# Start addresses of TensorE's streamed and loaded tiles, set by paddings in the second feed-forward network

## The chip, the cores and the metric

The kernel runs on one core of a Trainium2 chip. The metric is the time that the device takes for one execution, in microseconds (us). Smaller is better. The time of the kernel before is the median of three runs, 2021.54 us (2019.42 to 2022.19).

## The reference

Three stages follow one another. The input is 4 sequences of 3072 tokens with 256 channels, in float32.

```python
X = rfft(x, axis=1)                                   # 1: mixing along the sequence
Yr = Xr @ w_r - Xi @ w_i + b_r;  Yi = Xr @ w_i + Xi @ w_r + b_i
Y = soft_threshold(Yr, 0.01) + 1j * soft_threshold(Yi, 0.01)
y = irfft(Y, n=3072, axis=1)
xk, xr = mu * y + (1 - mu) * shifted(y)               # 2: first feed-forward network, 256 -> 1024 -> 256
out = sigmoid(xr @ w_rr) * (relu(xk @ w_k) ** 2 @ w_v)
h = out @ w_in                                        # 3: second feed-forward network, 256 -> 2048 -> 256
result = (h * clip(h + 3, 0, 6) / 6) @ w_out
```

## The kernel before

**How products are made.** A product of two float32 matrices is made of three matmuls: each operand is held as a rounded high part and the rest, a low part (names end in h and l, or in _hi and _lo), and high*high, low*high and high*low are added up in PSUM. A matmul consists of a weight load (LDWEIGHTS, 128 x 128 values of the operand that stays in the array) and the matmul proper (MATMUL), in which the other operand streams through, 256 or 512 columns. The load of the next matmul's weights runs beside the current matmul. So what is read at the same time is the streamed tile of one matmul and the weight tile of the one behind it.

**The stages in order.** Up to about 740 us the Fourier mixing (matmuls named s, mix, ia, ib) runs, from about 180 us on mixed with the first network (pr, pk, acc). From 740 us to 1000 us the first network runs alone, with the decoding of the second network's weights beside it. From 1000 us on the second network runs: its first tile of 512 tokens (of 24) with plain products (pi, 512 columns), and from 1043 us on 23 tiles by a scheme that replaces 8 block products by 7 (`u_s`: rq and cc, 256 columns), while the product with w_out (`u_o`: oacc, 256 columns) of an earlier unit is put in between.

**A turn of the second network.** A tile has 8 units; each turn (`turn`) advances four units in a fixed order. TensorE's part of a turn is 12 matmuls whose weights are sums of w_in (tiles sw0, sw1), then 9 whose weights are w_in itself (wi_hi, wi_lo), then the 24 matmuls of `u_o`, whose weights are the activations gh and gl and whose streamed tiles are wo_hi and wo_lo. What streams in the first 21 are the parts of the tile of tokens (xh, xl, allocated under the tags kh and kl, and the combinations th and tl). ScalarE and VectorE make a unit's gh and gl in its fourth turn, and `u_o` reads them in the turn after that. The order of all engines' work is written out by hand.

**Where tiles begin.** SBUF is handed out by pools in the order of the code; a pool takes a tile's place when the tile's tag is first used, and `pad` takes a few bytes with no use. Buffers of one tag, slices and halves that a matmul reads all lie whole multiples of 256 bytes apart, so one number, the address modulo 256, tells where all of a tag's operands begin. In the program before:

| read by | streamed tile: begins at | weight tile: begins at |
|---|---|---|
| mix (Fourier) | aw: 224 | Xh, Xl: 32 |
| ia (Fourier) | yh, yl: 224 | tt: 32 |
| pr, pk (first network) | kh, kl: 32 | wr, wk: 32 |
| acc (first network) | gh, gl: 32 | wv: 32 |
| pi (second network, first tile) | xh, xl (tags kh, kl): 32 | wi: 96 |
| rq, first 12 of a turn | xh, xl (tags kh, kl), th, tl: 32 | sw0, sw1: 32 |
| rq, cc, next 9 of a turn | xh, xl, th, tl: 32 | wi: 96 |
| oacc, 24 of a turn | wo: 224 | gh, gl: 32 |

The change touches `prep` (L536, the first use of the tags kh and kl), `split_s` (L679 to L682) and the allocation of the second network's weights (L967 to L971). All matmuls of the second network's later tiles are recorded under L824, those of pk, pr, acc, pi, mix and ia under L164.

Of the kernel before, what the change touches and what calls it, by code (L numbers as in the profile page):

```python
# [104 lines left out]
def fourier_mix_ffn_kernel(  # L105
# [33 lines left out]
    kb = ctx.enter_context(tc.tile_pool(name="kb", bufs=1))  # L139
# [5 lines left out]
    def pad(pool, n):  # L145

        pads.append(n)
        pool.tile([128, n // 4], F32, name=f"pad{len(pads)}")
# [73 lines left out]
    def decoder(jobs, stage):  # L222

        running = []
        for n in range(2 * len(jobs) + 5):
            for r in running:
                next(r, None)
            running = running[-3:]
            if n % 2 == 0 and n // 2 < len(jobs):
                w, *job = jobs[n // 2]  # L230
                running.append(w.decode(w.load(stage, *job), *job))
            yield
# [6 lines left out]
    with tc.manual_schedule(engines=order):  # L239
# [273 lines left out]
        def prep(i):  # L513

            if i:
                y = yt.pop(i)
                before, now = [(0, TOK, y)], [(0, TOK, y[:, :, N1:])]
            else:

                y1, y2 = ysb.pop(1), ysb.pop(2)  # L520
                before = [(0, 352, y1[:, :, 32:]), (352, TOK, y2)]
                now = [(0, 256, y1[:, :, 128:]), (256, TOK, y2)]
            for w in (1, 0):
                xf = kb.tile([128, 2, TOK], F32, tag="xf", bufs=1, name="xf")
                for a in range(2):
                    for lo, hi, y in before:
                        nc.scalar.activation(xf[:, a, lo:hi], y[:, a, 0 : hi - lo], AF.Copy, scale=omu[:, w, a : a + 1])
                yield
                for a in range(2):
                    for lo, hi, y in now:  # L530
                        o = xf[:, a, lo:hi]
                        nc.vector.scalar_tensor_tensor(
                            o, y[:, a, 0 : hi - lo], mus[:, w, a : a + 1], o, op0=ALU.mult, op1=ALU.add
                        )
                yield
                h = kb.tile([128, 2, TOK], F32R, tag="kh", bufs=3, name="kh")  # L536
                l = kb.tile([128, 2, TOK], F32R, tag="kl", bufs=3, name="kl")
                nc.scalar.activation(h, xf, AF.Copy)
                yield
                nc.vector.tensor_sub(l, xf, h.bitcast(F32))  # L540
                xs[i, w] = h, l
                yield

        def u_r(i):
            xr = xs.pop((i, 1))
            p = ptile("pr")
            for m in range(2):
                c = slice(128 * m, 128 * m + 128)
                three(
                    p[:, 512 * m : 512 * m + 512],  # L550
                    [((wr.hi[:, k, c], wr.lo[:, k, c]), (xr[0][:, k], xr[1][:, k])) for k in range(2)],
                )
            r = kb.tile([128, 2, TOK], F32, tag="r", bufs=2, name="r")
            nc.scalar.activation(r.rearrange("p a n -> p (a n)"), p, AF.Sigmoid)
            rs[i] = r

        def u_k(i, j):
            xk = xs[i, 0]
            p = ptile("pk")
            for m in range(2):  # L560
                c = slice(256 * j + 128 * m, 256 * j + 128 * m + 128)
                three(
                    p[:, 512 * m : 512 * m + 512],
                    [((wk.hi[:, k, c], wk.lo[:, k, c]), (xk[0][:, k], xk[1][:, k])) for k in range(2)],
                )
            g = kb.tile([128, 1024], F32, tag="g", bufs=2, name="g")
            h = kb.tile([128, 1024], F32R, tag="gh", bufs=3, name="gh")
            l = kb.tile([128, 1024], F32R, tag="gl", bufs=3, name="gl")
            nc.scalar.activation(g, p, AF.Relu)

            def rest():

                nc.scalar.activation(h, g, AF.Square)  # L573
                nc.vector.tensor_mul(g, g, g)  # L574
                nc.vector.tensor_sub(l, g, h.bitcast(F32))  # L575

            hv[i, j] = (h, l)
            return rest
# [95 lines left out]
        def split_s(sp, i):  # L674

            x = xt[i].rearrange("p k (t n) -> p k t n", t=2)
            flat = xt[i].rearrange("p k (t n) -> p (k t) n", t=2)
            tmp = {}
            h = kb.tile([128, 4, 256], F32R, tag="kh", bufs=3, name="xh4")  # L679
            l = kb.tile([128, 4, 256], F32R, tag="kl", bufs=3, name="xl4")  # L680
            th = sp.tile([128, 4, 256], F32R, tag="th", bufs=2, name="th")
            tl = sp.tile([128, 4, 256], F32R, tag="tl", bufs=2, name="tl")  # L682
            own = slice(0, 1), slice(2, 4)

            def four():
                t = tmp["t"] = sp.tile([128, 4, 256], F32, tag="t", bufs=1, name="xs")
                nc.vector.tensor_sub(t[:, 1], x[:, 0, 1], x[:, 0, 0])
                nc.vector.tensor_sub(t[:, 2], x[:, 1, 1], t[:, 1])
                nc.vector.tensor_sub(t[:, 3], x[:, 1, 1], x[:, 0, 1])
                nc.vector.tensor_sub(t[:, 0], x[:, 1, 0], t[:, 2])  # L690

            def high():
                for n in own:
                    nc.scalar.activation(h[:, n], flat[:, n], AF.Copy)

            def low():
                for n in own:
                    nc.vector.tensor_sub(l[:, n], flat[:, n], h[:, n].bitcast(F32))

            xt[i] = {n: (h[:, m], l[:, m]) for n, m in (("11", 0), ("21", 2), ("22", 3))}  # L700
            xt[i] |= {n: (th[:, m], tl[:, m]) for m, n in enumerate(("t4", "t1", "t2", "t3"))}
            return [
                (four, high),
                (low, lambda: nc.scalar.activation(th, tmp["t"], AF.Copy)),
                (lambda: nc.vector.tensor_sub(tl, tmp["t"], th.bitcast(F32)), None),  # L705
            ]
# [153 lines left out]
        for step, _ in enumerate(stream(first)):  # L860
# [4 lines left out]
            if step in SPLIT_MIX:  # L865
                w, staged, job = plain.pop(0)
# [4 lines left out]
            if step in DECODE:  # L871
                next(loads, None)
        fs = stream(later)
        preps = prep(0)
        for n in range(4):
            next(preps)
# [12 lines left out]
        def feed():  # L889

            nonlocal live_f
            live_f = live_f and next(fs, 0) is None
# [10 lines left out]
        def decode_to(n):  # L903

            nonlocal done2
            while done2 < n:
                next(jobs2, None)
                done2 += 1
# [34 lines left out]
        for n, (i, kind, j) in enumerate(units):  # L943
            if kind == "r":
                u_r(i)
            else:
                rest = u_k(i, j)
                lag.append((i, j))
            feed()
            ahead(i, 2 * (n % 5))  # L950
            next(loads, None)
            if n >= 2 and units[n - 2][1] == "k":
                if n == 3:
                    for _ in loads:
                        pass
                u_v(*lag.pop(0))
            if kind == "k":
                rest()
            next(loads, None)
            if n >= 2 and units[n - 2][1] == "k":  # L960
                feed()
            ahead(i, 2 * (n % 5) + 1)
            if not live_f:
                if jobs2 is None:
                    n0 = n
                    ff.close()
                    w2 = ctx.enter_context(tc.tile_pool(name="w2", bufs=1, side="right"))  # L967

                    wi = Weights(w2, w_in, 2, FF2, "wi")
                    pad(w2, 128)  # L970
                    wo = Weights(w2, w_out, 16, D, "wo")  # L971
                    stage = ctx.enter_context(ExitStack())
                    w3 = stage.enter_context(tc.tile_pool(name="w3", bufs=1, side="right"))

                    def stage2():
                        w = w3.tile([128, 1024], U32, tag="stw", bufs=3, name="stw2")
                        return w, w3.tile([128, 2, TOK], F32, tag="stt", bufs=3, name="stt2")

                    jobs2 = decoder(wi.jobs + wo.jobs, stage2)
                decode_to(37 * (n - n0 + 1) // (len(units) - n0))  # L980
# [3 lines left out]
        for n, (i, j) in enumerate(units):  # L984
            if i == 0:
                decode_to(max(done2 + 2, 2 * (j // 2 * 2 + 1) + 7, 2 * (8 + j) + 7))
                if j == 3:
                    decode_to(len(wi.jobs + wo.jobs) * 2 + 5)
                    stage.close()
                    sp = ctx.enter_context(tc.tile_pool(name="sp", bufs=1))  # L990
# [74 lines left out]
```

## Time and profile before

| | |
|---|---|
| median of three runs | 2021.54 us (2019.42 to 2022.19) |
| the profiled execution | 2019.82 us |
| its span, first to last instruction | 2018.1 us |
| TensorE busy with matmuls | 1970.9 us (98%), 13656 instructions |
| VectorE busy | 1417.5 us (70%) |
| ScalarE busy | 1228.0 us (61%) |
| mean granted TensorE clock | 0.990 |

A matmul's recorded duration holds its way through the array too, and overlaps the next one's. How fast TensorE works is read from the distance of starts: in the timeline by counting, or in a window by dividing its length by the number of matmuls that began in it. Where matmuls of one shape follow each other without a wait, a longer distance of starts shows as the same number of nanoseconds more in the mean duration of a group, which makes the groups' mean durations comparable.

### The profile page before, as it was taken

To read this page: it belongs to the slowest core of one execution; us is meant where nothing else is said; L and a number is where in the kernel's file an instruction comes from. 1 tells how busy PE (TensorE), PEld (TensorE's weight loads), DVE (VectorE), ACT (ScalarE), POOL (GpSimd) and SP (SyncE) were. 2 spreads that over 40 slices of the span, in tenths; PEclk is the share of its full clock that TensorE was granted. 3 is DMA by queue.
4 is the path that set the end of the run, shared out by engine and by line. 5 is a ranking of instruction groups with operands and counts; after the bars stand their busy time and mean duration, and the time that the engine had idled before them with its cause. 6 is when DMAs were issued, how large, how long until landed. Compare 5 with 4: busy or idle time off the path is not lost.

```text
span 2018.1 us, 33029 instructions
## 1 busy us (share of the span) xinstructions
PE 1970.9 (98%) x13656; PEld 1812.8 (90%) x13656; DVE 1417.5 (70%) x1721; ACT 1228.0 (61%) x1757; POOL 34.6 (2%) x63
## 2 busy tenths in 40 slices
PE   6789999999999999999999999999999999999998
PEld 4768987988798888777899999999999999999998
DVE  0756654565465658787878877788777887778776
ACT  2556555455445546666557766677667676676665
POOL 0000000000000000000000000000000000000000
PEclk8879999999999999999999999999999999999999
DMA  9675437444643342222101100011001010010100
GB/s 281 198 225 172 118 113 217 150 115 139 210 133 95 107 149 84 76 70 88 42 22 33 32 22 22 25 29 33 22 22 29 25 32 22 22 32 25 30 11 22
DMA packets 106712, 166.26 MB, mean 82 GB/s; under 512 B 12945, under 2 KB 62994, under 8 KB 106562
## 3 DMA queue, kind: packets, MB, share of 16 engines
q1 hardware_dynamic: 96034, 141.76, 22.6%
q0 software_dynamic: 10208, 22.13, 4.5%
q8 instruction: 107, 1.75, 0.4%
q14 instruction: 43, 0.35, 0.1%
q10 hardware_dynamic: 320, 0.26, 0.0%
HBM read 100.81 MB, written 63.31 MB: 81 GB/s over the span
## 4 chain that ended last, share of the span: by engine, by line
PE 81%; DVE 11%; ACT 5%; DMA 2%; issue 1%; ACTq 0%; SPq 0%; DVEq 0%; POOLq 0%
PE oacc L824 25%; PE rq L824 16%; PE acc L164 9%; PE pk L164 8%; PE cc L824 6%; PE mix L164 5%; PE ib L437 3%; PE s L332 3%; PE pr L164 2%; PE s L295 2%; DVE g L574 2%; DVE gl L575 2%; PE ia L164 1%; PE pi L164 1%; ACT gh L573 1%
## 5 line engine op out<-in xcount | busy, mean ns | idle before, releaser
L824 PE MATMUL oacc<-wo_hi,gl 128*128 128x256 f32 x1536 | 425.6, 277 | 1.2 <-DVE gl L765 1.2
L824 PE MATMUL oacc<-wo_hi,gh 128*128 128x256 f32 x1536 | 426.2, 277 | 0.0
L824 PE MATMUL oacc<-wo_lo,gh 128*128 128x256 f32 x1536 | 424.7, 276 | 0.0
L824 PEld LDWEIGHTS oacc<-wo_hi,gl 128*128 128x128 f32 x1536 | 289.2, 188 | 1.8 <-DVE gl L765 1.5
L824 PEld LDWEIGHTS oacc<-wo_hi,gh 128*128 128x128 f32 x1536 | 289.1, 188 | 0.2
L824 PEld LDWEIGHTS oacc<-wo_lo,gh 128*128 128x128 f32 x1536 | 288.5, 188 | 0.0
L756 DVE SCALAR_TENSOR_TENSOR g<-g,c 128x1024 f32<-128x1024 f32 x184 | 225.6, 1226 | 53.5 <-ACT g L752 53.3
L765 DVE TENSOR_TENSOR gl<-g,gh 128x1024 fp32r<-128x1024 f32 x184 | 225.3, 1224 | 50.0 <-ACT gh L762 47.2
L752 ACT ACTIVATE g<-c,half 128x1024 f32<-128x1024 f32 x184 | 212.4, 1154 | 4.9 <-DVE c L747 4.9
L824 PE MATMUL rq<-th,sw 128*128 128x256 f32 x1104 | 212.0, 281 | 0.1
L742 ACT ACTIVATE s<-rq 128x256 f32<-128x256 f32 x184 | 70.7, 384 | 220.1 <-PE rq L824 220.1
L762 ACT ACTIVATE gh<-g 128x1024 fp32r<-128x1024 f32 x184 | 193.9, 1054 | 1.6 <-DVE g L756 1.6
L746 DVE TENSOR_TENSOR c<-rq,s 128x512 f32<-128x512 f32 x184 | 126.8, 689 | 96.5 <-ACT s L742 96.4
L574 DVE TENSOR_TENSOR g<-g 128x1024 f32<-128x1024 f32 x96 | 117.4, 1223 | 106.3 <-ACT gh L573 106.1
L824 PEld LDWEIGHTS rq<-th,sw 128*128 128x128 f32 x1104 | 168.8, 189 | 0.3 <-ACT s L731 0.3
L164 PE MATMUL acc<-gl,wv_hi 128*128 128x512 f32 x384 | 151.2, 394 | 7.3 <-DVE gl L575 7.0
L164 PE MATMUL acc<-gh,wv_hi 128*128 128x512 f32 x384 | 155.6, 405 | 0.0
L824 PE MATMUL rq<-tl,sw 128*128 128x256 f32 x552 | 154.9, 281 | 0.6 <-DVE tl L705 0.6
L164 PE MATMUL pk<-kh,wk_hi 128*128 128x512 f32 x384 | 155.1, 404 | 0.0
L164 PE MATMUL acc<-gh,wv_lo 128*128 128x512 f32 x384 | 149.7, 390 | 0.0
L164 PE MATMUL pk<-kl,wk_hi 128*128 128x512 f32 x384 | 149.6, 390 | 0.0
L164 PE MATMUL pk<-kh,wk_lo 128*128 128x512 f32 x384 | 149.5, 389 | 0.0
(142 smaller groups left out, 4466.6 us busy)
## 6 DMA issues: line engine op xcount, KB each, us to landing
tt<-in_tab_dram POOLq DMA_DIRECT2D x40, 448.0 KB, 4.1
yt<-sc_y SPq DMA_DIRECT2D x23, 608.0 KB, 3.9
a<-in_x_dram SPq DMA_DIRECT2D x64, 192.0 KB, 4.2
sc_a<-s1sb SPq DMA_DIRECT2D x32, 384.0 KB, 4.0
a<-sc_a SPq DMA_DIRECT2D x48, 256.0 KB, 3.7
sc_b<-iasb SPq DMA_DIRECT2D x48, 256.0 KB, 3.9
a<-sc_b SPq DMA_DIRECT2D x64, 192.0 KB, 3.2
sc_y<-ysb SPq DMA_DIRECT2D x32, 384.0 KB, 3.1
```

Source lines behind the costliest of these rows:

```text
L164: nc.tensor.matmul(o, a, c, start=first and i == 0, stop=last and i == n - 1, **kw)
L295: nc.tensor.matmul(p[:N1, 512 * i : 512 * i + 512], f1, flat(a), start=True, stop=True)
L332: mm = lambda c, w, lhs, rhs: nc.tensor.matmul(p[:, c : c + w], lhs, rhs, start=True, stop=True)
L437: nc.tensor.matmul(p[:, q, et, i], lhs, fi, start=True, stop=True)
L574: nc.vector.tensor_mul(g, g, g)
L742: nc.scalar.activation(s[:, 3], q, AF.Copy)
L746: nc.vector.tensor_add(c[:, 1::2], two(rq), s[:, 0:2])
L752: nc.scalar.activation(g, c, AF.Relu, bias=half, scale=1.0 / 6.0)
L756: nc.vector.scalar_tensor_tensor(g, g, 1.0, tmp["c"], op0=ALU.min, op1=ALU.mult)
L762: nc.scalar.activation(h, tmp["g"], AF.Copy)
L765: nc.vector.tensor_sub(hg[i, j][1], tmp["g"], hg[i, j][0].bitcast(F32))
L824: return lambda: nc.tensor.matmul(o, lhs, rhs, start=start, stop=stop, skip_group_check=True)
```

## The change

Paddings alone are added or changed. No instruction, no order and no wait is changed.

```diff
@@ prep (first network), at the first use of the tags
                 yield
+                if not i and w:
+                    pad(kb, 192)
                 h = kb.tile([128, 2, TOK], F32R, tag="kh", bufs=3, name="kh")
                 l = kb.tile([128, 2, TOK], F32R, tag="kl", bufs=3, name="kl")
+                if not i and w:
+                    pad(kb, 64)
                 nc.scalar.activation(h, xf, AF.Copy)
@@ split_s (second network)
             l = kb.tile([128, 4, 256], F32R, tag="kl", bufs=3, name="xl4")
+            if i == 1:
+                pad(sp, 192)
             th = sp.tile([128, 4, 256], F32R, tag="th", bufs=2, name="th")
             tl = sp.tile([128, 4, 256], F32R, tag="tl", bufs=2, name="tl")
@@ weights of the second network
                     wi = Weights(w2, w_in, 2, FF2, "wi")
-                    pad(w2, 128)
+                    pad(w2, 192)
                     wo = Weights(w2, w_out, 16, D, "wo")
```

The first padding moves the tags kh and kl from 32 to 224; the second, 64 bytes behind them, makes 256 bytes in all, so that everything that lies behind keeps its place modulo 256. The third moves th and tl, and the temporaries behind them (xs, s, c), from 32 to 224. The pool w2 is filled from the top of memory, so that the larger padding moves wi from 96 to 32 and leaves wo at 224. Since the tags kh and kl serve both networks, the streamed tiles of pr and pk of the first network move to 224 too, while gh and gl, which acc streams, stay at 32.

## Rows read from the trace of the kernel before

**Rows 1.** The page's head and part 1: busy time, share of the span, instructions.

```profile
span 2018.1 us, 33029 instructions
PE 1970.9 (98%) x13656; PEld 1812.8 (90%) x13656; DVE 1417.5 (70%) x1721; ACT 1228.0 (61%) x1757; POOL 34.6 (2%) x63
```

**Rows 2.** Windows by stage: length, busy us (instructions) of each engine, clock, DMA share, GB/s.

```profile
1043.50:1090.00 46.50, 45.82 (x392) 45.42 (x391) 39.62 (x58) 31.79 (x50) 0.00 (x0) 1.00 0.08 24
1090.00:1995.00 905.00, 905.00 (x7804) 905.00 (x7804) 714.22 (x841) 622.17 (x973) 0.00 (x0) 1.00 0.09 26
```

**Rows 3.** Timeline of TensorE, one turn: start us, duration us, what ran, count.

```profile
1500.48 0.29 PE L824 MATMUL oacc<-wo_hi,gh 128*128 128x256 f32 x1
...
1501.07 0.28 PE L824 MATMUL oacc<-wo_lo,gh 128*128 128x256 f32 x1
...
1503.11 0.28 PE L824 MATMUL oacc<-wo_lo,gh 128*128 128x256 f32 x1
...
1505.70 0.29 PE L824 MATMUL oacc<-wo_hi,gh 128*128 128x256 f32 x1
```

**Rows 4.** Groups, 1100 to 1990 us: count, busy us, mean ns, idle before.

```profile
L824 PE MATMUL oacc<-wo_hi,gh 128*128 128x256 f32 x1364 | 378.3, 277 | 0.0
...
L824 PE MATMUL rq<-th,sw 128*128 128x256 f32 x1026 | 196.9, 281 | 0.0
...
L824 PE MATMUL cc<-xh,wi_lo 128*128 128x256 f32 x170 | 47.8, 281 | 0.0
```

**Rows 5.** Timeline of TensorE, a block of oacc in the second network's first tile.

```profile
1016.31 0.28 PE L824 MATMUL oacc<-wo_hi,gh 128*128 128x256 f32 x1
...
1019.02 0.28 PE L824 MATMUL oacc<-wo_lo,gh 128*128 128x256 f32 x1
```

**Rows 6.** Groups on TensorE, 112.2 to 115 us.

```profile
L164 PE MATMUL mix<-aw_hi,Xh 128*128 128x256 f32 x8 | 2.2, 276 | 0.0
```

**Rows 7.** Groups on TensorE, 573 to 575 us.

```profile
L164 PE MATMUL mix<-aw_hi,Xh 128*128 128x256 f32 x6 | 1.7, 281 | 0.0
```

**Rows 8.** Groups on TensorE, 1000 to 1002 us.

```profile
L164 PE MATMUL pi<-xh,wi_hi 128*128 128x512 f32 x4 | 1.6, 396 | 0.0
```

**Rows 9.** Timeline of TensorE, two blocks of pk in the first network.

```profile
754.69 0.39 PE L164 MATMUL pk<-kh,wk_hi 128*128 128x512 f32 x1
...
759.91 0.39 PE L164 MATMUL pk<-kl,wk_hi 128*128 128x512 f32 x1
```

**Rows 10.** Timeline of TensorE, a block of acc and two of pi.

```profile
1007.97 0.39 PE L164 MATMUL acc<-gh,wv_hi 128*128 128x512 f32 x1
...
1010.71 0.40 PE L164 MATMUL pi<-xh,wi_hi 128*128 128x512 f32 x1
...
1016.08 0.39 PE L164 MATMUL pi<-xl,wi_hi 128*128 128x512 f32 x1
```

**Rows 11.** Groups on TensorE, 740 to 930 us.

```profile
L164 PE MATMUL pk<-kl,wk_hi 128*128 128x512 f32 x118 | 45.9, 389 | 0.0
```

**Rows 12.** Timeline of TensorE behind a wait, in the turn that opens the third tile.

```profile
1081.53 0.39 PE L824 MATMUL rq<-tl,sw 128*128 128x256 f32 x1 [0.61 <-DVE tl L705]
...
1082.10 0.28 PE L824 MATMUL cc<-xh,wi_hi 128*128 128x256 f32 x1
...
1082.78 0.28 PE L824 MATMUL oacc<-wo_hi,gh 128*128 128x256 f32 x1
1082.90 0.28 PE L824 MATMUL oacc<-wo_hi,gl 128*128 128x256 f32 x1
```

**Rows 13.** Who TensorE waited for from 1043 us on: us, times, longest.

```profile
PE oacc L824 <- DVE gl L765: 1.2, 2, 0.7
PE rq L824 <- DVE tl L705: 0.6, 1, 0.6
```

**Rows 14.** Window of one turn with splits beside it, columns as in rows 2.

```profile
1526.58:1531.80 5.22, 5.22 (x48) 5.22 (x46) 4.84 (x7) 4.07 (x8) 0.00 (x0) 1.00 0.01 3
```

**Rows 15.** Page part 5, matmuls of pk over the whole run.

```profile
L164 PE MATMUL pk<-kl,wk_hi 128*128 128x512 f32 x384 | 149.6, 390 | 0.0
```

## The prediction

> **What bounds the kernel now.** I read the page's head first: TensorE is busy for 98% of a span of 2018.1 us, VectorE for 70% and ScalarE for 61% [rows 1]. The windows by stage then show where that share is complete: from 1090 to 1995 us TensorE is busy for 905.00 of 905.00 us, at a granted clock of 1.00 (the 2.4 GHz level), with 7804 matmuls of 256 columns [rows 2]. That is one matmul per 116.0 ns. The list of waits says the same: from 1043 us on TensorE waited three times, 1.8 us in all [rows 13]. So in 45% of the run nothing but the distance of matmul starts sets the time, and a nanosecond there counts 7804 times.
>
> That distance is not one number. In a turn of 5.22 us (1500.48 to 1505.70), the 18 steps of oacc from 1501.07 to 1503.11 take 2.04 us, 113.3 ns each, while the rest of the turn's 45 steps is slower [rows 3]. The groups show it as mean durations: 277 ns for oacc, 281 for rq and cc [rows 4]. The block of oacc at 1016 us has 23 steps in 2.71 us, 117.8 each [rows 5]. I call these the **fast and the slow cadence**, 113.3 and 117.8 ns; as the duration grows with the distance of starts, they are the 276 and the 281 of the groups [rows 6, 7].
>
> **What the addresses have to do with it.** While one matmul streams, the next one's weights are loaded. I put the streamed tile's address minus the next weight tile's, modulo 256, beside each step (addresses from the table in the text):
> - difference 192: oacc and mix (224 and 32), ia, and rq and cc on wi (32 and 96: -64, the same 192). These have both cadences: mix 276 in one stretch, 281 in another [rows 6, 7]; cc 281 in the mean of the turns [rows 4], but from 1082.10 to 1082.78 six steps of it take 113.3 each [rows 12]. Each holds for as long as such pairs follow each other: all of oacc's later steps in a turn, 23 steps at 1016 us.
> - difference 0, 256 columns: the 11 steps of a turn from one sw matmul to the next, and the step from the last cc (streams at 32) to gh (32). The mean on sw is 281 [rows 4], and these pairs throw TensorE out of the fast cadence: behind the six steps of cc at 113.3 comes the pair with difference 0, and the next step, of oacc, is 120 [rows 12].
> - difference 0, 512 columns (pk, pr, acc): 23 steps in 5.22 us, 227.0 each, a duration of 389 ns [rows 9, 11]. That is twice 113.3, nothing lost.
> - difference 192, 512 columns (pi): 23 steps in 5.37 us, 233.5 each, 396 ns [rows 8, 10].
>
> That (32, 96) and (224, 32) show the same two cadences is my reason to take the difference, not either address, for what counts. No row shows 512 columns at (224, 32); I price it by pi.
>
> **The change part by part.** It adds no instruction and no wait. What moves is the pairs.
> 1. *Turns of the second network.* Sums of pairs: now 33 of 45 at difference 192 and 12 at 0; afterwards all 45 at 192. If nothing throws TensorE out, the cadence is one of the two throughout. Which? What enters it. After each wait in this stage the steps settle at the fast one: behind the wait for tl at 1081.53 the 32/96 pairs run at 113.3 [rows 12], and behind both waits at the end of the run (for gl [rows 13]) oacc does. The slow cadence came behind blocks of 512 columns without a wait [rows 5, 10]. The wait for tl stands at the start of the third tile, and what it waits for is not touched. So I take fast: 7804 x 113.3 = 884.4 instead of 905.00, **-20.6 us**. Between 1043.5 and 1090 us lie 392 more such steps [rows 2]; at 116.0 - 113.3 = 2.7 ns less each: -1.0 us. But the wait for tl ends with VectorE's chain, which does not get shorter, so TensorE waits that much longer: +1.0. Were the slow cadence kept: 7804 x 117.8 = 919.3, +14.3 us, and 392 x 1.8 = +0.7 before 1090.
> 2. *Who is next.* A turn of 45 x 113.3 is 5.10 us. In the fullest turn of a tile, with the next tile's splits beside it, VectorE is busy for 4.84 us and ScalarE for 4.07 [rows 14]. gh and gl are read a turn after they are made, so TensorE stays the bound, by 0.26 us in that turn and by more in the others.
> 3. *pr and pk of the first network*, which share the tags: from difference 0 to 192 with 512 columns, 227.0 to 233.5. 24 tiles x 5 x 12 = 1440 matmuls x 6.5 = 9.4 us, if all were at 227 now. Over the whole run pk has a mean of 390 where the undisturbed stretch has 389 [rows 11, 15], so some steps are longer already, those of blocks behind other shapes: 1 of 7 ns, a seventh of the price. I take **+8.5 us**, between 8.1 and 9.4. The lower bound is 0 (512 columns at 224/32 keep 227), the upper 9.4.
> 4. *acc behind pk.* acc keeps difference 0 but is entered from another phase. Behind pi its 12 steps take 2.74 us (1007.97 to 1010.71) [rows 10] against 12 x 227.0 = 2.72. Some 42 blocks of acc follow pk or pr directly: 42 x 0.02 to 0.03 = **+1 us**. mix and ia behind pk may come out at the fast cadence instead of the slow one: at most 18 blocks of 24 steps x 4.5 ns, -2 us; I take 0 and keep the end.
> 5. *The first tile* (pi, oacc): pi keeps its difference, oacc too. The temporaries xs, s and c at 224 and the streams of DMA change nothing that I can price: 0.
>
> Sum: -20.6 - 1.0 + 1.0 + 8.5 + 1 = -11.1 us, 0.55%. Against the profiled execution of 2019.82 that is 2008.7; the median of the runs shown stands 1.7 higher, at 2021.54, which would give 2010.4. I say 2009.
>
> **A rule against it.** mix runs at 276 and at 281 ns with the very same tiles [rows 6, 7], so the addresses alone do not set the cadence. The Trainium skill goes further: TensorE: Matmul & The Clock Gate, section "Part 2: What happens when you issue a matmul", says that TensorE has two independent read ports, one for the streamed operand and one for the weights, and that loading the next weights takes no bandwidth from the running matmul; by that, paddings would do nothing, 2021.5. The trace speaks against it only by the grouping above.
>
> **The rivals.**
> - *Addresses do nothing.* The cadence would follow from the order of the matmuls alone. For it: rows 6 and 7. Against: the same cc is fast or not by the pairs before it [rows 4, 12], and 512 columns take 389 ns in pk and 396 in pi, same shape, same clock [rows 8, 11]. Time 2021.5. This holds too if both cadences take turns so that gains and the cost of pk cancel.
> - *Slower: the slow cadence holds.* The turns enter at 117.8 and, as no pair of difference 0 throws them out any more, stay there; the waits that reset it come too early or not at all. It decides from the point where more than about a third of the turns are slow: 20.6 gained with all fast, 14.3 lost with all slow, 9.5 lost in pk and acc, so nothing is left at (20.6 - 9.5) / (20.6 + 14.3) = 0.32. All slow: 2021.5 + 14.3 + 0.7 + 9.5 = 2046. A milder form, the cost of pk with unchanged turns, is 2031. For it: the long slow stretches of mix and of oacc at 1016 us [rows 5, 7]; against: every wait in this stage was followed by the fast cadence [rows 12].
> - *No cost in the first network.* 512 columns at (224, 32) keep 227.0, because the address counts and not the difference: -20.6 and up to -2 for mix, 2019.8 - 22.6 = 1997 to 2001. Against: pi's 233.5 held for 24 steps at the same difference [rows 10].
>
> **How the numbers follow.** Forecast (fast turns, cost in pk) 0.59, 2004 to 2014. No cost 0.13, 1996 to 2004. Nothing or cancelled 0.11, 2018 to 2023. Slower 0.17, 2026 to 2046. Leaving out the slower cases and what lies beyond, the range is 1996 to 2023. A change of less than 0.2% (4 us) is about what a measurement of this kernel can't tell from none. Faster 0.72, same 0.11, slower 0.17.
>
> **What would show it.** Right: rq and cc at 276 instead of 281, oacc at 276, a turn of 5.10 us, 1090 to 1995 us shortened to about 884; pk and pr at 396 instead of 389; the wait for tl near 1080 us longer by up to 1.0. Wrong: rq and cc at 281 throughout (slow), or oacc at 281 as well; new waits of TensorE on VectorE's c or gl in the turns with splits (step 2); pk at 389 (step 3).

## The result, and the profile after

The changed kernel takes 0.9914 of the time of the kernel before (95% interval 0.9894 to 0.9933), about 2003 us against 2020.9; 2009.0 was predicted. Two of its executions, 2040.0 and 2037.9 us, are left out of that ratio; over all ten executions of this program (five here, five in e0 below) the mean is 2010.3 us. The profiled one, 2040.0, ran the second network at the slow cadence from 1088 us on; the other has no profile and is taken to have done so from its time. I therefore show two profiles: one of the same program at the fast cadence (a second measurement of it, 2003.2 us, ratio 0.9910, 0.9897 to 0.9924), and the one at the slow cadence.

At the fast cadence: the page's head and part 1 (busy us, share, instructions), beside [rows 1]:

```profile
span 1999.0 us, 33029 instructions
PE 1951.9 (98%) x13656; PEld 1784.6 (89%) x13656; DVE 1416.6 (71%) x1721; ACT 1226.7 (61%) x1757; POOL 34.5 (2%) x63
```

A window of the turns (columns as in [rows 2]), first at the fast, then, in the other profile, at the slow cadence:

```profile
1090.00:1974.00 884.00, 884.00 (x7802) 884.00 (x7802) 713.60 (x841) 623.59 (x975) 0.00 (x0) 1.00 0.09 26
```

```profile
1090.00:1974.00 884.00, 884.00 (x7508) 884.00 (x7507) 690.45 (x814) 599.54 (x939) 0.00 (x0) 1.00 0.09 26
```

A window also counts the two matmuls that reach into it from outside, so that these are 884 us / 7800 = 113.3 ns and 884 / 7506 = 117.8 ns per matmul; before it was 116.0 [rows 2]. TensorE is complete in both, at the full granted clock. The groups on TensorE from 1100 to 1980 us answer [rows 4]; fast, then slow:

```profile
L830 PE MATMUL oacc<-wo_hi,gh 128*128 128x256 f32 x1384 | 382.0, 276 | 0.0
L830 PE MATMUL rq<-th,sw 128*128 128x256 f32 x1032 | 192.4, 276 | 0.0
L830 PE MATMUL cc<-xh,wi_lo 128*128 128x256 f32 x172 | 47.5, 276 | 0.0
```

```profile
L830 PE MATMUL oacc<-wo_hi,gh 128*128 128x256 f32 x1329 | 373.4, 281 | 0.0
L830 PE MATMUL rq<-th,sw 128*128 128x256 f32 x996 | 191.0, 281 | 0.0
L830 PE MATMUL cc<-xh,wi_lo 128*128 128x256 f32 x166 | 46.6, 281 | 0.0
```

All three kinds share one duration now, 276 or 281, where before oacc had 277 and the other two 281. The timeline of one fast turn, first matmul to first matmul, is 5.10 us long (before: 5.22 [rows 3]):

```profile
1500.65 0.39 PE L830 MATMUL rq<-th,sw 128*128 128x256 f32 x2
...
1505.75 0.39 PE L830 MATMUL rq<-th,sw 128*128 128x256 f32 x2
```

Which of the two it is can change at a wait. In the profile at the slow cadence the turns before 1085 us still run fast. Its timeline of TensorE, the six steps of cc of one turn, then the wait for tl, then the same six of the next turn:

```profile
1081.53 0.28 PE L830 MATMUL cc<-xh,wi_hi 128*128 128x256 f32 x1
...
1082.21 0.28 PE L830 MATMUL oacc<-wo_hi,gh 128*128 128x256 f32 x1
...
1087.64 0.38 PE L830 MATMUL rq<-tl,sw 128*128 128x256 f32 x1 [0.95 <-DVE tl L711]
...
1088.21 0.28 PE L830 MATMUL cc<-xh,wi_hi 128*128 128x256 f32 x1
...
1088.92 0.28 PE L830 MATMUL oacc<-wo_hi,gh 128*128 128x256 f32 x1
```

Six steps in 0.68 us (113.3 each) ahead of the wait, in 0.71 us (118) behind it. Pairs of the same tags with the same difference, the same clock, no wait within either six: only what lies between them, a wait, differs. From there the slow cadence holds for some 940 us, up to the end of the run, where TensorE waits for gl twice: behind the first of these waits the next 22 steps have a mean of 114.1 ns, behind the second 21 steps 117.8.

The first network: the page's row of pk over the whole run answers [rows 15], 394 for 390:

```profile
L164 PE MATMUL pk<-kl,wk_hi 128*128 128x512 f32 x384 | 151.5, 394 | 0.5 <-DVE kl L544 0.5
```

Who TensorE waited for (us, times, longest), from 740 to 1010 us, first in the trace of before, then in that at the fast cadence, the latter with the stage from 1043 us on, which answers [rows 13]:

```profile
PE acc L164 <- DVE gl L575: 7.0, 9, 1.4
```

```profile
PE acc L164 <- DVE gl L579: 4.7, 6, 1.2
...
PE oacc L830 <- DVE gl L771: 1.2, 2, 0.7
PE rq L830 <- DVE tl L711: 0.9, 1, 0.9
```

With the slower pk the waits of acc are 2.3 us shorter. The second network got no new wait; the one for tl is 0.3 us longer.

### The profile page after: what moved, and what is told of

It is laid out like the page before. It is cut to its first block, busy times and chain, and to the rows that moved or that the text cites. A ratio compares the mean times of both kernels' runs of the same rounds, so it can differ in the third digit from the quotient of the medians.

```text
span 2038.2 us, 33029 instructions
## 1 busy us (share of the span) xinstructions
PE 1992.3 (98%) x13656; PEld 1825.9 (90%) x13656; DVE 1418.6 (70%) x1721; ACT 1226.2 (60%) x1757; POOL 34.9 (2%) x63
## 4 chain that ended last, share of the span: by engine, by line
PE 83%; DVE 10%; ACT 4%; DMA 2%; issue 1%; SPq 0%; ACTq 0%; DVEq 0%; POOLq 0%
PE oacc L830 25%; PE rq L830 15%; PE acc L164 9%; PE pk L164 9%; PE cc L830 6%; PE mix L164 5%; PE ib L437 3%; PE s L332 3%; PE pr L164 2%; PE s L295 2%; DVE g L578 2%; DVE gl L579 1%; PE ia L164 1%; PE pi L164 1%; ACT gh L577 1%
## 5 line engine op out<-in xcount | busy, mean ns | idle before, releaser
L830 PE MATMUL oacc<-wo_hi,gl 128*128 128x256 f32 x1536 | 431.3, 281 | 0.9 <-DVE gl L771 0.9
L830 PE MATMUL oacc<-wo_hi,gh 128*128 128x256 f32 x1536 | 431.1, 281 | 0.0
L830 PE MATMUL oacc<-wo_lo,gh 128*128 128x256 f32 x1536 | 431.1, 281 | 0.0
L830 PEld LDWEIGHTS oacc<-wo_lo,gh 128*128 128x128 f32 x1536 | 294.4, 192 | 0.0
```

The costliest lines, as they stand in the source:

```text
L830: return lambda: nc.tensor.matmul(o, lhs, rhs, start=start, stop=stop, skip_group_check=True)
```

## The experiments

All ratios are against the kernel before on the same chip. "Difference" is the prediction's: streamed tile's address minus the next weight tile's, modulo 256.

### e0_again: the changed kernel once more

No edit. It asks whether further executions show the same two cadences, and gives a profile at the fast one.

> The changed kernel once more. Theory A (two settled cadences; a wait of TensorE starts one of them, by chance, and it holds until the next wait): every execution of it lies near 2003 us or near 2038 us, none between except one that changes cadence at the waits near 1050 and 1086 us; a profiled execution near 2003 shows the turns of the second network at 5.10 us with rq, cc and oacc at 276 ns, one near 2038 shows 5.30 us and 281 ns. Theory B (something outside the kernel slows some executions): the longer executions are longer in every stage, the Fourier stage and the first network too, and the distance of starts in the second network lies between 113.3 and 117.8 ns.

Measured: 2003.18 us (2000.72 to 2004.39), ratio 0.9910 (0.9897 to 0.9924); all five, by their times, at the fast cadence. Its profile is the fast one above. In it the price of the first network can be split, by comparing the distance of each start to the next with that of the same matmul in the trace of before, from the first pr to the first pi: pk's steps +6.6 us, pr's +1.5, acc's +1.0, together +9.1; mix and ia -0.5; and, from 740 us on, the distances that hold a wait of acc -3.1. That is 5.5 of the 7.0 us by which this stretch is longer in the second trace; the rest, 1.5 us, lies mostly in gaps before 740 us, and was not followed further.

### e1_wk224 and e2_wk96: is it the difference or the address?

e1 takes the changed kernel and moves wr and wk to 224, so that pk and pr are back at difference 0, both ends now at 224. e2 takes the kernel before and moves wr and wk to 96: difference 192 from addresses (32, 96) that have nothing to do with 224. In both wv stays at 32.

```diff
@@ e1, on the changed kernel: weights of the first network
+        pad(kw_p, 192)
         wr = Weights(kw_p, w_rr, 2, D, "wr")
         wk = Weights(kw_p, w_k, 2, FF1, "wk")
+        pad(kw_p, 64)
         wv = Weights(kw_p, w_v, 8, D, "wv")
@@ e2, on the kernel before: the same places
+        pad(kw_p, 64)
...
+        pad(kw_p, 192)
```

> The changed kernel with the first network's weights wr and wk at 224 too (wv stays at 32), so that pr and pk are back at difference 0. Theory A (the difference modulo 256 counts): pk at 389 ns and 227.0 ns per start as before the change, where it is 395 in the changed kernel; the executions at the fast cadence are 8 to 10 us shorter than the changed kernel's, near 1994 us, the ones at the slow cadence near 2030 us. Theory B (the address 224 of the streamed tile alone costs): pk stays at 395 ns and the times of the changed kernel remain, near 2003 and 2038 us.

> The kernel before with wr and wk at 96 and nothing else moved (kh and kl stay at 32): pr and pk at difference 192 from another pair of addresses. Theory A (difference): pk at 393 to 398 ns, 233.3 per start, and 8 to 10 us more than the kernel before, near 2030 us, with little spread, since the second network's turns stay as they were (5.22 us). Theory B (only the streamed tile's place at 224 costs): 389 ns and the time of the kernel before, 2021 us.

Measured: e1 2001.59 us (1999.89 to 2003.17), ratio 0.9900 (0.9886 to 0.9914); e2 2023.67 (2022.0 to 2026.71), ratio 1.0014 (1.0005 to 1.0023). The group of pk from 740 to 930 us, e1 and then e2, beside 389 before [rows 11]:

```profile
L164 PE MATMUL pk<-kl,wk_hi 128*128 128x512 f32 x116 | 45.2, 390 | 0.0
```

```profile
L164 PE MATMUL pk<-kl,wk_hi 128*128 128x512 f32 x116 | 45.9, 395 | 0.0
```

The durations follow the difference: 390 at (224, 224), 395 at (32, 96), as 394 at (224, 32) and 396 for pi at (32, 96) [rows 8]. That is settled. The price is not what the durations make it: e2 has all of the longer steps of pk and pr and costs 2.8 us, not 8 to 10, and e1 gave back less than 2 of them, within the intervals of both measurements. The waits from 740 to 1010 us say where the rest is, e1 and then e2:

```profile
PE acc L164 <- DVE gl L581: 5.9, 7, 1.4
```

```profile
PE acc L164 <- DVE gl L577: 4.8, 6, 1.2
```

With pk slow (e2, changed kernel) 4.8 and 4.7 us, with pk at difference 0 (before) 7.0, with e1 between. A likely reason for e1, not tested by itself: its acc enters from difference 192 and leaves at 64, and became slower itself (394 for 391 in the group of acc).

### e3_d128, e4_d64, e5_d0: other differences throughout

Three versions in which all pairs of the second network have one difference: 128 (streams at 160), 64 (streams at 96) and 0 (wi and wo at 32 on the kernel before). e4 has the edit of e3 with 64, 192, 64, 64 and 128 in place of its 128, 128, 128, 128 and 64.

```diff
@@ e3, on the changed kernel: paddings of kh and kl, of th and tl, of wo
-                    pad(kb, 192)
+                    pad(kb, 128)
...
-                    pad(kb, 64)
+                    pad(kb, 128)
...
-                pad(sp, 192)
+                pad(sp, 128)
...
-                    pad(w2, 192)
+                    pad(w2, 128)
                     wo = Weights(w2, w_out, 16, D, "wo")
+                    pad(w2, 64)
@@ e5, on the kernel before: weights of the second network
                     wi = Weights(w2, w_in, 2, FF2, "wi")
-                    pad(w2, 128)
                     wo = Weights(w2, w_out, 16, D, "wo")
+                    pad(w2, 192)
```

> As the changed kernel, but all that streams in the second network begins at 160 (kh, kl, th, tl, wo), weights at 32: difference 128. Theory A says that the cadence depends on the difference, and has not seen 128. If 128 has one settled cadence only, all executions agree; at 113.3 ns per start that is 2000 to 2004 us less or plus what pk does at 128 (0 to 10 us), at a slower one, 118 to 121 ns, 2040 to 2065 us. Theory B (addresses do nothing, chance at the waits alone): executions at 2003 and at 2038 us as with the changed kernel.

> As the changed kernel, but all that streams in the second network begins at 96: difference 64. At 128 the steps of rq, cc and oacc had a mean of 118.6 ns and the time was 2043 to 2054 us. Theory A: 64 has its own settled cadence or cadences; if one of them is at 113.3 and is the only one, all executions are near 2003 us, else 2035 to 2055 us. Theory B (addresses do nothing): 2003 or 2038 us as the changed kernel.

> The kernel before with wi and wo at 32, so that all that streams in the second network and all its weights begin at 32: difference 0 in all 45 pairs of a turn; the first network is not touched. Theory A: the 512-column matmuls lose nothing at difference 0 (227.0 per start, twice 113.3), the 11 pairs of sw in a turn never settled at 113.3 with 256 columns; I expect 118 to 120 ns per start, a turn of 5.31 to 5.40 us, 2038 to 2055 us, without two kinds of executions. If 0 is as good at 256 columns as at 512, the turn is 5.10 us and the time near 1999 us.

Measured: e3 2049.08 us (2043.01 to 2054.37), ratio 1.0134 (1.0107 to 1.0161); e4 2038.19 (2036.26 to 2038.66), 1.0088 (1.0073 to 1.0103); e5 2051.14 (2050.79 to 2055.01), 1.0153 (1.0136 to 1.0170). The window of the turns, one of each kernel in this order:

```profile
1090.00:1974.00 884.00, 884.00 (x7452) 884.00 (x7451) 685.96 (x810) 596.23 (x934) 0.00 (x0) 1.00 0.09 26
```

```profile
1090.00:1974.00 884.00, 884.00 (x7508) 884.00 (x7507) 690.64 (x815) 601.11 (x940) 0.00 (x0) 1.00 0.09 26
```

```profile
1090.00:1974.00 884.00, 884.00 (x7369) 884.00 (x7369) 678.30 (x796) 589.75 (x922) 0.00 (x0) 1.00 0.09 26
```

With two taken off each count: 118.7, 117.8 and 120.0 ns per matmul. e3's executions fall into two groups, near 2043.5 and near 2054.3; the window is of one of the first, and what sets the second apart is open. Paddings alone move the same program by some 50 us (e1 to e5), so the rival "addresses do nothing" is out, whatever the order. Difference 192 is the only one of the four at which 113.3 was seen to hold; 64 gives the 117.8 that 192 has at its slow cadence. That it is the difference and not the streamed tile's address shows for 256 columns too: tiles that begin at 32 take 120.0 with weights at 32 (e5), and 113.3 or 118 with weights at 96 (cc in [rows 12] and in e7 below). Differences 64 and 128 were run from one pair of addresses each. With 512 columns the order is another: pk has 389 ns at difference 0, 392 at 64, 395 at 128 and 394 to 395 at 192.

### e7_sw96: one odd pair per turn

On the kernel before, sw0 and sw1 move to 96. Of a turn's 45 pairs one then has difference 0 (last cc to gh), one 128 (last oacc to sw), and 43 have 192.

```diff
@@ on the kernel before: allocation of sw0, sw1, and split_s
                     sp = ctx.enter_context(tc.tile_pool(name="sp", bufs=1))
+                    pad(sp, 64)
...
+            if i == 1:
+                pad(sp, 192)
             th = sp.tile([128, 4, 256], F32R, tag="th", bufs=2, name="th")
```

> The kernel before with sw0 and sw1 at 96 and nothing else moved (th, tl at 32): in a turn all pairs are at difference 192 but two, one at 0 (the last cc before gh) and one at 128 (the last oacc before sw). Theory A (a pair off 192 throws TensorE from one cadence into the other, once per pair): the cadence changes at most twice a turn and the same way in every turn, so that there is one time without chance: with oacc fast and the 21 others slow 45 steps take 24 x 113.3 + 21 x 117.8 = 5.19 us a turn and 2016 us, with all fast 5.10 us and about 2001 us, with all slow 5.30 us and 2036 us. Theory B (the tile that begins at 224 is what is quick): 281 ns on rq and cc and 276 on oacc, 2021 us.

Measured: 2019.03 us (2017.07 to 2022.8), ratio 0.9997 (0.9988 to 1.0006): no difference, though 43 of 45 pairs have the difference that can run at 113.3. The timeline of TensorE shows why, here from the odd pair at 1504.06 on:

```profile
1503.35 0.28 PE L826 MATMUL cc<-xh,wi_hi 128*128 128x256 f32 x1
...
1504.06 0.29 PE L826 MATMUL oacc<-wo_hi,gh 128*128 128x256 f32 x1
...
1504.53 0.28 PE L826 MATMUL oacc<-wo_hi,gl 128*128 128x256 f32 x1
...
1506.68 0.28 PE L826 MATMUL oacc<-wo_lo,gh 128*128 128x256 f32 x1
```

Ahead of it the six steps of cc take 0.71 us, 118 each; behind it four take 0.47 (118), and the 19 from 1504.53 on 2.15, 113.2 each. So the one pair at difference 0 takes TensorE from the slow cadence to the fast one, and the pair at 128 at the turn's end takes it back. It works the other way too. In the trace of before, the turn that [rows 12] shows had entered oacc from a fast cc. Its oacc, and then that of the next turn, whose cc was slow again:

```profile
1083.02 0.28 PE L824 MATMUL oacc<-wo_lo,gh 128*128 128x256 f32 x1
1085.49 0.28 PE L824 MATMUL oacc<-wo_lo,gh 128*128 128x256 f32 x1
...
1088.34 0.28 PE L824 MATMUL oacc<-wo_lo,gh 128*128 128x256 f32 x1
1090.72 0.28 PE L824 MATMUL oacc<-wo_lo,gh 128*128 128x256 f32 x1
```

21 steps in 2.47 us (117.6) behind the fast cc, 21 in 2.38 us (113.3) behind the slow one. The trace of before has the same in the first tile, whose five blocks of oacc each stand behind one pair at 0 (the last pi, at 32, before gh, at 32; a pair at 128, from oacc to pi, lies between two blocks as well): the block of [rows 5] has 117.8, the next one, behind the same pi, settles at 113.3 (18 steps in 2.04 us):

```profile
1022.53 0.28 PE L824 MATMUL oacc<-wo_lo,gh 128*128 128x256 f32 x1
...
1024.57 0.28 PE L824 MATMUL oacc<-wo_lo,gh 128*128 128x256 f32 x1
```

The five have means of 117.8, 114.1, 117.8, 114.1 and 117.8; in the changed kernel, where that pair is at 192, all five lie between 113.4 and 113.8. A single pair at difference 0 seems to swap the two, rather than to end the fast one, as the prediction had it. In e7 the means of the groups, 281 on rq and 277 on oacc, are also what theory B says; against it stand the slow blocks of oacc here, which stream from 224 as well. And taken with each matmul's own weights, all 45 pairs of e7 would be at 192; that the cadence changes at the last cc speaks for the next matmul's weights.

### e8_waits and e9_before_waits: does a wait choose the cadence?

VectorE makes one gl per tile seven more times, so that TensorE has to wait for it once in each tile. e8 does that with all pairs of the second network at 192 (on e6, below), e9 with the kernel before.

```diff
@@ u_s, low()
                 nc.vector.tensor_sub(hg[i, j][1], tmp["g"], hg[i, j][0].bitcast(F32))
+                for w in [1024] * 6 + [32 * i] if j == 2 else []:
+                    nc.vector.tensor_sub(hg[i, j][1][:, 0:w], tmp["g"][:, 0:w], hg[i, j][0][:, 0:w].bitcast(F32))
```

> The kernel of e6_tags (second network at difference 192 throughout, first network as before), in which VectorE makes one gl of each tile seven more times (six whole, some 1.22 us each as in the trace of e6_tags, and one part that is 0.04 us longer from tile to tile), so that TensorE has to wait for gl about once in a tile, 22 times in all, each time at another moment of its work. Nothing else is added, and a part of VectorE's work stands in the program more than once. Theory, chance: what comes after a wait draws one of the two cadences and keeps it until the next wait. Then some of the 22 stretches between waits run at 113.3 ns a step (turn 5.10 us) and some at 117.8 (turn 5.30), at least 3 of each, and a stretch does not change by itself. Rival, the prediction's step: behind a wait the fast cadence always settles; then all 22 stretches show 113.3. Rival, the execution: the cadence is set once for a whole execution; then all stretches are alike, whichever it is. Time: VectorE is busy for 33.0 of a tile's 40.8 us and gets 7.4 to 8.2 more, so 1998 plus waits of 0.5 to 3 us in each of 22 tiles: 2010 to 2065.

> The kernel before with the same repeated work on VectorE as in e8_waits. Its turns hold 12 pairs at difference 0. In the trace of before the turn behind the wait for tl was fast in cc and slow in oacc, and from the second turn on the pattern was the usual one. Theory: the pairs at difference 0 bring the same pattern back after each wait, within one or two turns; all stretches between waits then end in turns of 5.22 us, with rq and cc slow and oacc fast, and no stretch keeps another cadence. Rival: the draw of a wait is kept here as well; then stretches with oacc at 117.8 or cc at 113.3 last until the next wait. Time: turns of 5.22 us leave VectorE 41.8 us a tile for 33.0 plus 7.4 to 8.2, so waits are shorter than in e8_waits: 2024 to 2070.

Measured: e8 2165.7 us, e9 2166.9 us, one execution each. Both are above what was expected: the waits are not 0.5 to 3 us but mostly over 4 (why I had them too short was not followed up), and behind each of them the granted clock is 0.50 for a while (last section). The waits of e8 from 1043 us on, longest group:

```profile
PE oacc L829 <- DVE gl L770: 100.1, 23, 4.9
```

What counts are the stretches between waits. Windows of 30 us of e8, each well inside one stretch, three stretches in sequence and two later:

```profile
1279.00:1309.00 30.00, 30.00 (x267) 30.00 (x266) 23.04 (x28) 19.85 (x32) 0.00 (x0) 1.00 0.07 19
1327.00:1357.00 30.00, 30.00 (x257) 30.00 (x257) 22.04 (x27) 18.73 (x31) 0.00 (x0) 1.00 0.07 19
1375.00:1405.00 30.00, 30.00 (x267) 30.00 (x266) 23.90 (x29) 20.33 (x32) 0.00 (x0) 1.00 0.07 19
...
1903.00:1933.00 30.00, 30.00 (x257) 30.00 (x256) 22.96 (x28) 19.63 (x33) 0.00 (x0) 1.00 0.07 19
1951.00:1981.00 30.00, 30.00 (x267) 30.00 (x266) 22.87 (x28) 19.83 (x32) 0.00 (x0) 1.00 0.07 19
```

267 matmuls are 113.3 ns apart, 257 are 117.8. Of the 22 long stretches from 1090 us on, 14 were fast and 8 slow. Counted turn by turn, none changed within itself. So the cadence belongs neither to the program nor to the execution: it is open again at each wait, as in a draw, and then stays until the next. The prediction's step, that the fast one settles behind a wait, is out. Three stretches of e9:

```profile
1279.00:1309.00 30.00, 30.00 (x261) 30.00 (x260) 23.26 (x27) 19.61 (x31) 0.00 (x0) 1.00 0.07 19
...
1664.00:1694.00 30.00, 30.00 (x260) 30.00 (x260) 23.26 (x29) 20.00 (x32) 0.00 (x0) 1.00 0.07 19
...
1903.00:1933.00 30.00, 30.00 (x261) 30.00 (x260) 23.34 (x29) 19.75 (x31) 0.00 (x0) 1.00 0.07 19
```

Here all 22 return to 116.0 ns: with pairs at difference 0 in each turn the same pattern comes back. That is why the kernel before shows no such spread, and the changed one does.

### e6_tags and e11_tags_again: the second network alone

The second network as in the changed kernel, the first as before: kh and kl are made 64 elements longer, and the second network uses them from element 48 (192 bytes) on.

```diff
@@ on the changed kernel, without its paddings in prep
+    def ktile(tag, at, q, name=None):
+        t = kb.tile([128, 1088], F32R, tag=tag, bufs=3, name=name or tag)
+        return t[:, at : at + 1024].rearrange("p (q n) -> p q n", q=q)
...
-                h = kb.tile([128, 2, TOK], F32R, tag="kh", bufs=3, name="kh")
-                l = kb.tile([128, 2, TOK], F32R, tag="kl", bufs=3, name="kl")
+                h, l = ktile("kh", 0, 2), ktile("kl", 0, 2)
...
+            h, l = ktile("kh", 48, 4, "xh4"), ktile("kl", 48, 4, "xl4")
```

> The change for the second network alone: buffers of the tags kh and kl are 256 bytes longer, the first network uses them from 32 on as before the change, the second from 224 on; all else as in the changed kernel. So pr, pk and acc stay at difference 0 with no odd pair at their borders, and all 45 pairs of a turn are at 192. Theory A (the difference counts; the changed kernel lost some 5 us in the first network): pk at 389 ns; executions at the fast cadence 4 to 6 us shorter than the changed kernel's 2003 us, near 1998 us; the others near 2033 us. Theory B (what was lost in the first network has another cause, the start or the transfers): 2001 to 2004 us.

> The kernel of e6_tags once more, for more executions. Theory, chance: its second network has the same pairs as the changed kernel, so among five or more executions some may come out near 2034 (all turns behind the wait for tl at 117.8 ns: 1998.8 plus 7804 steps times 4.5 ns) or anywhere between, where a wait on the way draws anew; most near 1998.8, as 8 of 10 of the changed kernel did. Rival: the place of the waits in this program makes the fast cadence certain: all within 1996 to 2002.

Measured: 1998.79 us (1996.98 to 1999.87), ratio 0.9894 (0.9879 to 0.9909), and again 1998.02 (1996.91 to 1998.54), ratio 0.9892 (0.9875 to 0.9908). All eight executions lie below every one of the changed kernel. In e6 pk is at 389 again (740 to 930 us), and so are the waits of acc near the 7.0 of before:

```profile
L168 PE MATMUL pk<-kl,wk_hi 128*128 128x512 f32 x119 | 46.3, 389 | 0.0
...
PE acc L168 <- DVE gl L578: 6.7, 8, 1.4
```

Against the kernel before on the same chip the second network by itself is worth 20.8 us (e6) and 22.6 us (e11), the whole change 17.8 (e0), so that the first network's part of it costs 3.0 to 4.8 us. This version beats the kernel before clearly; that it beats the changed one rests on the eight times and on pk, for the intervals of the ratios overlap. That it can't fall into the slow cadence is not shown: it has the same pairs, and e8, built on it, fell into it 8 times.

## Why the prediction was right, and where it was wrong

For the executions at the fast cadence the sign, the pairs as the cause and the range held. 2003 lies 6 us below the 2009 that was said, a little below its forecast's own range of 2004 to 2014 and inside the one that "no cost" had been given, and the executions at the slow cadence lie above the whole range. That most executions were fast was in part luck (2).

1. *Turns at the fast cadence, -20.6.* Right in size: 7802 steps x 2.67 ns (116.00 - 113.33) are -20.8, and the start of the same matmul in both traces shifts by 20.7 us from 1090 us to 1990. All three kinds at 276, the turn at 5.10. The -1.0 + 1.0 around the wait for tl was a little too careful: the starts shift by a net -0.5 from 1043.5 to 1090 us, and the wait for tl is only 0.3 us longer (0.9 for 0.6), not 1.0.
2. *"After each wait in this stage the steps settle at the fast one."* This step failed. It rested on three waits, all of which happened to be followed by fast steps; one of them even led into a slow oacc. "The slow cadence came behind blocks of 512 columns without a wait" held for three of the five blocks of oacc in that tile; the one 5.6 us later in the same trace settled at 113.3 (e7). In the changed kernel the very wait that I named, for tl, was followed by some 940 us of slow steps, and e8 has 14 fast and 8 slow draws. The time came out on the fast side because most executions drew it so: by their times, 20 of the 22 that are known of the changed kernel, e1, e6 and e11, whose second networks have the same pairs. The rival "the slow cadence holds" was therefore no alternative theory but the other outcome of the same program. Its price was right: 2046 said with 9.5 in the first network; with 3.0 to 4.8 it is 2040 to 2041, and 2040.0 and 2037.9 were measured.
3. *VectorE next, TensorE stays the bound.* Right: no new wait from 1043 us on, although a turn became 0.12 us shorter.
4. *pr, pk and acc, +9.5.* The durations were right (394 to 395 where 396 was said; steps +9.1 us in e0), and also that a difference of 192 costs them and not an address (e2). The sum was wrong: the path through the first network also holds waits of acc for gl, which VectorE sets. Steps that get longer ahead of such a wait shorten it: -3.1 us in e0, with -0.5 from mix and ia. By the times 3.0 to 4.8 us were left; the two traces differ by 7.0 there, 1.5 of it in gaps that none of these terms has. I had read the waits from 1043 us on only, and costed every step of the first network as if TensorE were as complete there as in the second. The row of the waits with its 7.0 us was to be had before.
5. *First tile, 0.* It was -0.4 us: pi and oacc keep their differences, but the pair between them moved from 0 to 192, and oacc's slow blocks became fast.

"Addresses do nothing" fell with e5 and e3. "No cost in the first network" gave 1997 to 2001 and so came close in time, but for a reason that is not there: pk did get longer.

The rule of the Trainium skill (TensorE: Matmul & The Clock Gate, "Part 2: What happens when you issue a matmul") that loading the next weights takes no read bandwidth from the running matmul does not hold here as a statement on time: with nothing but start addresses changed, a matmul of 256 columns took 113.3, 117.8, 118.7 or 120.0 ns, and moving the weight tiles alone took pk from 389 to 395 (e2).

What stays open: what in TensorE or its memory makes the difference count, and what in a wait decides the draw. Only the rate was seen, 14 to 8 in one program, whose waits were long and nearly all had the clock change of the last section behind them. Whether short waits draw at the same rate is not settled: the changed kernel's wait for tl, 0.9 us in both profiles, shows that they can draw either, and the 20 of 22 executions are the only count.

## What to carry to other kernels

Where matmuls of 256 columns follow each other without a gap, take the distance of starts apart by pairs (what streams now, what is loaded for the next) and by the operands' addresses modulo 256, before you call TensorE full: 6% lay between the best and the worst of four differences here. When a step gets longer ahead of a wait, take the wait off its price, and read the waits of every stage that the change touches, not only of the one it is meant for. A state that was seen after every one of three waits is a sample of three; a kernel that rests on it should be timed in many executions.

## What the runs showed of the hardware

| difference, modulo 256 | 256 columns, ns per matmul | 512 columns, duration of pk, ns |
|---|---|---|
| 0 | 120.0 (e5) | 389 (before, e5), 390 (e1) |
| 64 | 117.8 (e4) | 392 (e4) |
| 128 | 118.7 (e3) | 395 (e3) |
| 192 | 113.3 or 117.8 | 394 (changed), 395 (e2) |

Difference 0 is the best for 512 columns and the worst for 256. With 256 columns, 0, 64 and 128 were run with weights at 32 alone, 192 also with weights at 96. Two cadences for the very same pairs, each stable over more than 900 us and open again at a wait, I had not expected.

The clock behind the long waits of e8 was not expected either: windows around one of them (the last column but two is the granted clock).

```profile
1264.60:1270.60 6.00, 1.74 (x16) 1.55 (x14) 5.83 (x7) 0.38 (x1) 0.00 (x0) 0.87 0.00 0
1270.80:1273.80 3.00, 3.00 (x15) 3.00 (x15) 3.00 (x6) 1.54 (x2) 0.00 (x0) 0.50 0.06 12
1274.00:1277.00 3.00, 3.00 (x21) 3.00 (x20) 2.85 (x3) 2.36 (x4) 0.00 (x0) 0.70 0.46 166
1279.00:1309.00 30.00, 30.00 (x267) 30.00 (x266) 23.04 (x28) 19.85 (x32) 0.00 (x0) 1.00 0.07 19
```

TensorE stood still for most of the first window, waiting for gl; when work came back, it was granted 0.50 (1.2 GHz) in the next 3 us, some 213 ns from start to start, and later 1.00 (2.4 GHz) again. Behind this wait 24 steps took 100 ns more each and the first some 200 more, 2.6 us together. Over all 23 such waits it was 1.4 to 3.0 us each, 49 us together, counted from the steps behind each. With 104 us for the waits themselves (the distance of starts across each, less one step) and some 13 for the eight slow stretches of up to 359 steps x 4.5 ns that makes 166 us, where e8 lies 167 above e6 (2165.7 - 1998.8). So behind a wait that lets the clock fall, the wait was not the whole price.
